# Two linear-attention layers on one core: four products multiplied straight out of PSUM, without filler products, under a new table of order

## The chip, the core and the metric

The kernel runs on one core of one Trainium2 chip. The metric is device time in microseconds (us) of one execution. The core has five instruction queues that matter here: TensorE (PE in the profile, with its weight loads as PEld), ScalarE (ACT), VectorE (DVE), GpSimd (POOL) and SyncE (SP, which here only issues DMAs). Products land in PSUM; everything else works in SBUF.

## The reference

The input `x` is 2048 tokens of 512 values, with 32 heads of 16. Two kinds of layers follow each other twice, each behind a layernorm without weights and with a residual add:

```python
x = A_x
x = x + _A_ref(_layernorm(x), ...)     # layer 0, A
x = x + _B_ref(_layernorm(x), ...)     # layer 0, B
x = x + _A_ref(_layernorm(x), ...)     # layer 1, A
x = x + _B_ref(_layernorm(x), ...)     # layer 1, B
```

A cuts the tokens into 4 segments of 512. In each it does causal softmax attention, and mixes in what a running memory of the earlier segments gives. B has no mask and no segments:

```python
pq = jnp.einsum('bhsd,hdf->bhsf', q, w_phi)
pk = jnp.einsum('bhsd,hdf->bhsf', k, w_phi)
phi_q = jnp.concatenate([_softmax(pq), _softmax(-pq)], axis=-1)
phi_k = jnp.concatenate([_softmax(pk), _softmax(-pk)], axis=-1)
kv = jnp.einsum('bhsf,bhsd->bhfd', phi_k, v)
z = jnp.einsum('bhsf->bhf', phi_k)
num = jnp.einsum('bhqf,bhfd->bhqd', phi_q, kv)
den = jnp.einsum('bhqf,bhf->bhq', phi_q, z)[..., None] + 1e-06
o = num / den                           # then @ wo
```

So B's queries need the sums `kv` and `z` over all 2048 tokens before any of them can be multiplied out. That is why the kernel ends with a stage that has only the queries of the second layer B in it.

## The kernel before

**Tiles.** The tokens lie in 16 tiles of 128 (tile `t`), four to a segment or chunk `c`. `X`, the running sum, stays in SBUF from the first load to the last store. PSUM is used through a few buffers; the four large ones of a pool `pD`, 128 x 1024 in f32 each (`D` in the profile), hold nearly all products that somebody must then copy, exponentiate, multiply or add.

**Order.** The program is written as a graph of operations. Each has the tiles it reads and writes, and one engine or two that may run it. `Graph.place` gives every operation a place in one total order, an engine, and every tile a buffer. All three come out of a table, the string `ORDER`, which is packed in base 85 and says nothing to a reader. `emit` then writes each engine's program in that order, with a semaphore wait wherever an operation needs another engine's result or a buffer that another engine still uses. Each engine runs its own program strictly in order, so an instruction that waits holds all that stand behind it on its engine. SP's queue holds the DMA transposes (line 383) and the stores (line 387) in the same manner.

**The stages.** Layer A of the first layer goes segment by segment (`a_proj`, `a_att`, `out_proj`), each followed by `b_keys`, which adds the segment's keys to `kv` and `z` (products "KV", the running sum on DVE, and at the last one `Rkv` of line 943). Then `b_query` of each chunk of the first layer overlaps layer A of the second. The second `b_query` has nothing behind it: it is the end of the program, from about 424 us on.

**`b_query`.** For a chunk of four tiles PE makes the query products, ACT exponentiates them into `EQ` (lines 366, "qexp"), PE makes the denominators, and DVE and ACT turn them into the weights `AB`. Then each tile has a chain of its own: PE's numerators `N` in PSUM; their multiplication by the weights on DVE into `Tm`; the sum of the two halves of `Tm`, on DVE or POOL ("nadd"); a transpose of that, mostly by a DMA from SP; the output products on PE (line 356); the residual add into `X` out of PSUM on DVE (line 926); and, in the second layer, the store. The multiplication has two forms:

```python
if (L, t) in COPIED:
    Ns = self.T(self.p2, "T")
    self.act(lambda Ns=Ns: Ns.t[:], lambda N=N: N.t[:], ACT.Copy, 1024, [N], [Ns], label="Nev")
    v(lambda e, ...: e.tensor_tensor(shape(Tm.t[:]), shape(Ns.t[:]), w(), ALU.mult), 600, ...)    # line 1087
else:
    v(lambda e, ...: e.tensor_tensor(shape(Tm.t[:]), shape(N.t[:]), w(), ALU.mult), 1131, ...)    # line 1090
```

In the first, ACT copies `N` to SBUF as bf16 (through a helper, so its line in the profile is 366), and DVE multiplies from there. In the second, DVE reads `N` out of PSUM itself. `COPIED` has all 16 tiles of the second layer and tiles 0 to 3 of the first. Tiles 0 and 15 of the second layer (`PE_T`) have no sum and no DMA: PE transposes and adds their two halves, and an eviction follows. Tiles 14 and 15 (`SOLO`) have output products of their own; the others go in pairs.

**Other lines that the prediction names.** Line 341 and line 356 are PE's products, 356 those of the projections and of `kv`. Lines 374 and 375 are copies out of PSUM by ACT or DVE. Lines 590 and 591 are a tile's layernorm statistics, line 605 a small step of the same. Line 878 divides layer A's products out of PSUM, and line 882 adds the memory's part, on DVE or POOL ("oadd"). Line 795 is a step of the memory's part, line 1007 weights the values for `kv`, line 650 belongs to the feature map of A's keys, line 541 is a step of the gates at the start. Line 662 is the warm-up of PE at the start.

**Filler products.** `keep` (line 671 on) makes two products of a constant with itself into a buffer of `pD`, which nobody reads. Six of them stand among the other operations of the last stage; the row of their twelve products is at line 678.

Of the kernel before, what the change touches and what calls it, by code (L numbers as in the profile page):

```python
# [16 lines left out]
D = 512  # L17
H = 32
# [294 lines left out]
class Kernel:  # L313
# [149 lines left out]
    def T(self, pool, cls):  # L463
        return Tile(pool, cls)
# [206 lines left out]
    def keep(self):  # L671

        D = self.T(self.pD, "S")

        def fn(e):
            for hf in range(2):
                r = self.onesb[64 * hf:64 * hf + 64, :]
                ins = e.matmul(D.t[:, 512 * hf:512 * hf + 512], r, r[:, None, :].to_broadcast([64, 4, 128]), start=True, stop=True, tile_position=(64 * hf, 0))
            return ins
        self.g.op({"pe": (215.0, fn)}, [self.R("onesb")], [D], label="keep", rows=64)  # L680

# [421 lines left out]
    def build(self):  # L1103
        R = self.R
# [9 lines left out]
        for L in range(2):  # L1114
            if L == 0:
# [7 lines left out]
                g0 = next(o for o in self.g.ops[n0:] if o.label == LATER[0])  # L1123
# [4 lines left out]
            for s in range(NSEG):  # L1128
# [5 lines left out]
                for i0 in (0, 2):  # L1134
                    t = s * 4 + i0
# [11 lines left out]
        for _ in range(N_KEEP):  # L1147
            self.keep()
# [21 lines left out]
COPIED = {(L, t) for L in range(2) for t in range(16) if L or t < 4}  # L1170
HALVED = set()
N_WARM = 16
N_KEEP = 6
# [4 lines left out]
c-rlG1GFYtlWpMm8fDwIZQHhO+qP}n=q}rAn`L%ab=S-MZdXt9|9jTVd+W_wli$7hWu9{~V#kghk(u{qfQFD5k^n<eNCu6dF*JchkQ&lJIzUJPDIpbPg!E7oN<u9FC<w  # L1178
Ko4iE%^fKpHz3PEA02xXuw)P<(d44Oj=XbG*LHMD`Y&<-j=d*}cip$HU(%1{OBK_18jouD&xfpSnDia}MV2F0NS)Q1Xi4X(otXaJ|+4%~#ia2n3Q1*i@ZG+czP&<$!pI
J}45L4ko`&;uNtg<jAT`okyK7y7_V7!I>wB#eLvm;<BW9Gr)K&>Py~Y`6rM;R;-ZOwb-PLvFYWqag>}g0%1{-iEO-2Hu1B;RE;(+F=L$4D&-OOpS9P9>&M7a3VCsMmP@  # L1180
^zzv)a1E4O}!-dch7r|m!0{I{d41}AQ6*^%WOpBed3w{q#@RV}G=a>RhVggKv@!=jkfcr2Bp3z4z2<qct_!xrWQ%HmwKY<3g43<I?Ooz#E2xP#-m>iShExe5x@k@9JUq
N~t4_$F6bi<z53o~J690wr~2?ia0jg7GhT3ikjpgZ=!6_5pMV;y`>D<KHC!xjjIrq~CwK{I?GKfp)u1x&%Im>s@`V4Mt}!wj5>{V)UzV-f6&q4*7a1{+`sJcjkq8=K=d
_$_9|7MKkIXW?vYjrkFg(ZXgZfL*975w^h|)CyZ-Ps)xtup8yXT-YB6;8xfMyP!LT!H4(}#)E>m8>YfE_!y@{F&u(<aTDah@9=xfjfHR(48<8x9K&!Fj>ddg6iZ-9EQR
# [90 lines left out]
```

## Time and profile before

| | |
|---|---|
| median of 3 runs | 463.37 us (462.33 to 463.4) |
| the profiled execution | 462.93 us, of which the profile's span is 461.2 |
| mean granted clock of TensorE in it | 0.998 |
| busy: PE, DVE, ACT, POOL | 437.7, 416.2, 420.3 and 80.1 us |
| HBM read and written | 6.32 MB and 2.10 MB |

Busy time is the time in which an engine had an instruction running. The page's slices give the same over time, a fortieth of the span (11.5 us) to a digit:

```profile
PE   8989899899999999998899999999999999998896
...
DVE  6989998898889999898999899998899889998896
ACT  4999999899999998789699999999999999878991
POOL 2402021101221211102532031130221023110020
```

Rows of the groups (lines) have: line, engine, operation, what it writes and reads with its shape, count; then busy time and the mean of one in ns; then the engine's idle time before such instructions and who ended it. Rows of a timeline have: start, duration, engine, line, operation, tiles; and in square brackets the wait before it with the instruction that ended it. Rows of a chain have: start, duration, and the instruction or transfer that held the next one.

### The profile page before, as it was taken

How to read it: one execution, taken by the hardware profiler on the slowest of the kernel's cores; microseconds unless marked ns; L12 is line 12 of the kernel's file. 1: busy time of each engine (PE TensorE's matmuls, PEld its weight loads, DVE VectorE, ACT ScalarE, POOL GpSimd, SP SyncE). 2: the span in 40 equal slices, each digit the busy share in tenths (PEclk: the TensorE clock that was granted, in tenths of full speed). 3: DMA queues.
4: the chain of work that ended last, by engine and by line, in shares of the span. 5: the costliest groups of instructions: out<-in, count | busy, mean ns of one | idle time of the engine just before them, and what ended most of it. 6: DMA issues, size and time to landing. Idle time of an engine off the chain costs nothing.

```text
span 461.2 us, 25354 instructions
## 1 busy us (share of the span) xinstructions
PE 437.7 (95%) x11716; PEld 295.6 (64%) x11716; DVE 416.2 (90%) x807; ACT 420.3 (91%) x542; POOL 80.1 (17%) x160
## 2 busy tenths in 40 slices
PE   8989899899999999998899999999999999998896
PEld 4456667667776776675456677677677677666553
DVE  6989998898889999898999899998899889998896
ACT  4999999899999998789699999999999999878991
POOL 2402021101221211102532031130221023110020
PEclk9999999999999999999999999999999999999999
DMA  8554642552233322100243443264113321200357
GB/s 247 127 150 80 127 63 37 75 96 54 50 46 54 46 40 36 37 3 4 48 54 78 71 85 72 49 96 61 26 39 49 50 39 27 48 14 1 50 121 180
DMA packets 90058, 30.37 MB, mean 66 GB/s; under 512 B 76640, under 2 KB 89952, under 8 KB 89952
## 3 DMA queue, kind: packets, MB, share of 16 engines
q1 hardware_dynamic: 89520, 28.48, 33.3%
q8 instruction: 92, 1.51, 1.4%
q10 hardware_dynamic: 432, 0.27, 0.2%
q14 instruction: 14, 0.11, 0.1%
HBM read 6.32 MB, written 2.10 MB: 18 GB/s over the span
## 4 chain that ended last, share of the span: by engine, by line
PE 48%; ACT 40%; DVE 6%; DMA 3%; issue 2%; SPq 0%
PE D L356 31%; ACT p L366 21%; PE D L341 15%; ACT pF L366 13%; ACT pE L366 5%; DMA p<-p 2%; PE D L662 2%; DVE X L926 1%; DMA X<-in_A_x_dram 1%; DVE p L1090 1%; DVE p L375 1%; DVE stats L590 1%; ACT pS L366 1%; DVE p L611 0%; DVE pK L375 0%
## 5 line engine op out<-in xcount | busy, mean ns | idle before, releaser
L366 ACT ACTIVATE p<-D 128x1024 bf16<-128x1024 f32 (+2 forms) x224 | 216.0, 1004 | 13.5 <-PE D L356 9.7
L366 ACT ACTIVATE pF<-D 128x896 bf16<-128x896 f32 x128 | 116.7, 940 | 2.8 <-PE D L341 2.5
L341 PE MATMUL D<-pK,pQ 64*128 64x256 bf16 (+3 forms) x1536 | 112.9, 243 | 4.1 <-ACT pF L366 1.0
L341 PEld LDWEIGHTS D<-pK,pQ 64*128 64x128 bf16 x1536 | 55.2, 94 | 40.7 <-ACT pF L366 5.4
L341 PE MATMUL D<-pV,pF 64*128 64x34 bf16 x1024 | 73.8, 175 | 0.4 <-ACT p L366 0.4
L341 PE MATMUL D<-pW,pF 64*128 64x34 bf16 x1024 | 71.3, 175 | 0.0
L341 PEld LDWEIGHTS D<-pV,pF 64*128 64x128 bf16 x1024 | 55.3, 93 | 2.3 <-ACT p L366 0.7
L341 PE MATMUL D<-pV,p 64*128 64x34 bf16 x1024 | 53.3, 176 | 0.3 <-issue 0.2
L366 ACT ACTIVATE pE<-D 128x768 bf16<-128x768 f32 x64 | 52.3, 831 | 1.4 <-PE D L341 1.0
L341 PEld LDWEIGHTS D<-pW,pF 64*128 64x128 bf16 x1024 | 51.9, 93 | 0.9
L341 PE MATMUL D<-pW,p 64*128 64x34 bf16 x1024 | 52.1, 176 | 0.0
L598 POOL TENSOR_SCALAR rstd<-mv 128x1 f32<-128x1 f32 x60 | 16.1, 272 | 205.9 <-DVE mv L591 205.5
L341 PEld LDWEIGHTS D<-pV,p 64*128 64x128 bf16 x1024 | 47.0, 93 | 3.3 <-issue 0.9
L341 PE MATMUL D<-tri,two 64*128 64x128 bf16 (+1 forms) x384 | 46.7, 234 | 0.4 <-issue 0.4
L341 PEld LDWEIGHTS D<-pW,p 64*128 64x128 bf16 x1024 | 45.2, 93 | 1.3
L590 DVE BATCH_NORM_STATS2 stats<-X 128x6 f32<-128x512 bf16 x64 | 42.9, 680 | 3.0 <-DMA X<-in_A_x_dram 2.5
L341 PE MATMUL D<-pV,pE 64*128 64x34 bf16 x512 | 44.9, 175 | 0.4 <-issue 0.4
L926 DVE TENSOR_TENSOR X<-X,D 128x1024 bf16<-128x1024 bf16 (+1 forms) x36 | 39.4, 1095 | 5.7 <-PE D L356 5.0
L341 PE MATMUL D<-pW,pE 64*128 64x34 bf16 x512 | 42.5, 175 | 0.1
L985 DVE TENSOR_REDUCE pS<-p 128x64 f32<-128x1024 bf16 (+1 forms) x36 | 38.8, 1088 | 1.8 <-ACT p L366 1.8
L375 DVE CAST p<-D 128x512 bf16<-128x512 f32 x48 | 31.1, 683 | 6.3 <-PE D L356 6.1
L356 PE MATMUL D<-WB_o,p 64*128 64x512 bf16 (+1 forms) x288 | 33.0, 353 | 2.7 <-issue 1.3
(115 smaller groups left out, 988.9 us busy)
## 6 DMA issues: line engine op xcount, KB each, us to landing
pW<-pV SPq DMA_DIRECT2D x16, 136.0 KB, 3.1
out_dram<-X SPq DMA_DIRECT2D x7, 256.0 KB, 2.8
X<-in_A_x_dram SPq DMA_DIRECT2D x3, 512.0 KB, 6.1
pX<-in_B_wqkv_dram SPq DMA_DIRECT2D x3, 512.0 KB, 4.6
p<-p SPq DMA_TRANSPOSE x76, 2.8
pX<-p SPq DMA_TRANSPOSE x54, 3.2
WA_k<-in_A_wk_dram SPq DMA_DIRECT2D x2, 256.0 KB, 6.3
WA_q<-in_A_wq_dram SPq DMA_DIRECT2D x2, 256.0 KB, 7.0
```

The costliest lines, as they stand in the source:

```text
L341: ins = e.matmul(out_ap, lhsT, rhs, start=st, stop=sp, tile_position=(basep(lhsT), basep(out_ap)))
L356: ins = e.matmul(out_ap, lhsT[64 * hf:64 * hf + 64], rhs[64 * hf:64 * hf + 64], start=k == 0 and i == 0, stop=k == 1 and i == len(lists[hf ...
L366: return self.g.op({"act": (dur, lambda e: e.activation(out_ap(), in_ap(), func, scale=scale))}, reads, writes, opens, label=label)
L375: "dve": ((340 if fast else n / 0.96 + 65), lambda e: e.tensor_copy(out_ap(), in_ap()))}
L590: v(lambda e: e.bn_stats(self.stats[:, t, :], self.X[:, t, :]), 602, [R("X", t)], [R("st", t)], label="bn")
L598: v(lambda e: e.tensor_scalar(rs, self.mv[:, t, 1:2], LN_EPS, None, op0=ALU.add), 170, [R("mv", t)], [R("rstd", t)], eng="pool", label="rstd")
L662: ins = e.matmul(D.t[c0:, r0 * 8:r0 * 8 + n], r[:, c0:], ones(r, n), start=True, stop=True, tile_position=(r0, c0))
L926: self.v(lambda e: e.tensor_tensor(X(), X(), src(), ALU.add), 65 + 512 * n / 0.96, pr + xr, xr, label="res")
L985: fn = lambda e, sgn=sgn, eo=eo, Z=Z, n=n: e.tensor_reduce(Z.t[:, 0:64 * n].rearrange("p (k s h) -> p k s h", k=n, s=2)[:, :, sgn, :], eo( ...
L1090: v(lambda e, N=N, Tm=Tm, w=w, shape=shape: e.tensor_tensor(shape(Tm.t[:]), shape(N.t[:]), w(), ALU.mult), 1131, [N, AB[(0, 0)], AB[(0, 1) ...
```

## The change

`COPIED` loses every fourth tile of the second layer: 3, 7, 11 and 15. Their numerators are multiplied by DVE out of PSUM, and four copies of ACT are gone. `keep` and its six calls are gone. The table `ORDER` is a new one. It moves instructions on all engines, most by a few places, and changes the engine of some: of the sums of line 1093, eight go from DVE to POOL and one comes back; of the sums of line 882, four go and two come back; several copies out of PSUM change between ACT and DVE, as many in one direction as in the other. In all, DVE has 798 operations in place of 807, ACT 540 in place of 544, POOL 165 in place of 156, and PE six fewer. From the place of `keep` on, a line of the new kernel has a number lower by 11, from `COPIED` on by more.

```diff
@@ -667,17 +667,6 @@
...
-    def keep(self):
-
-        D = self.T(self.pD, "S")
-
-        def fn(e):
-            for hf in range(2):
-                r = self.onesb[64 * hf:64 * hf + 64, :]
-                ins = e.matmul(D.t[:, 512 * hf:512 * hf + 512], r, r[:, None, :].to_broadcast([64, 4, 128]), start=True, stop=True, tile_position=(64 * hf, 0))
-            return ins
-        self.g.op({"pe": (215.0, fn)}, [self.R("onesb")], [D], label="keep", rows=64)
...
@@ -1144,8 +1133,6 @@
...
-        for _ in range(N_KEEP):
-            self.keep()
         self.g.place(self.pools, ORDER)
...
@@ -1167,72 +1154,71 @@
...
-COPIED = {(L, t) for L in range(2) for t in range(16) if L or t < 4}
+COPIED = {(L, t) for L in range(2) for t in range(16) if L == 1 and t % 4 != 3 or L == 0 and t < 4}
...
-N_KEEP = 6
...
 ORDER = """
-c-rlG1GFYtlWpMm8fDwIZQHhO+qP}n=q}rAn`L%ab=S-MZdXt9|9jTVd+W_wli$7hWu9{~V#kghk(u{qfQFD5k^n<eNCu6dF*JchkQ&lJIzUJPDIpbPg!E7oN<u9FC<w
...
+c-rlH1(Y4fl4U@0Gl-d)nVFfHnVFfHnVFdxZ80<00$VbOWsq#imNZo@>96f?&w9MOXJ^mZ>h6N9sK^^PZp6#?`o)I?kOq=NU8o23p#e06M$j0V00Tl(Xa-3jDFCE^gg_
...
```

Where the prediction shows rows of an order, they are an engine's instructions in the order of its program: line, operation, tile written and tiles read, shape, and xN for N like ones in a row.

More of the change, by code (lines that the diff above doesn't have):

```diff
@@ L1180 @@
[L1180 to L1183, printed above, removed]
@@ L1233 @@
[L1233 to L1235 removed]
+c-rlH1(Y4fl4U@0Gl-d)nVFfHnVFfHnVFdxZ80<00$VbOWsq#imNZo@>96f?&w9MOXJ^mZ>h6N9sK^^PZp6#?`o)I?kOq=NU8o23p#e06M$j0V00Tl(Xa-3jDFCE^gg_
+7g0#ZS0NC}CcDinokP#y9@4JZc1As^(2vQQJ6LknmLt)MlufwoWrN<ukk2kk*Z0VoLNp#s!`oS>l;l!ii37&<^M$N{;bA{2p8s05Xv3e<)=PzE}}F*puq;1XPhc+d$H8
```

110 lines of the change are left out of this document (56 added, 54 removed).

## The prediction

> **What bounds the kernel now.** I read the page's busy times first, then the chain of waits, then busy time by stretch, then the timelines of DVE, ACT and SP where the chain leaves PE and ACT.
>
> ```profile
> PE 437.7 (95%) x11716; PEld 295.6 (64%) x11716; DVE 416.2 (90%) x807; ACT 420.3 (91%) x542; POOL 80.1 (17%) x160
> PE 48%; ACT 40%; DVE 6%; DMA 3%; issue 2%; SPq 0%
> ```
>
> Three engines are above 90%, and the chain changes between PE and ACT all the time: no engine alone is the bound. So the question is stage by stage which one is full.
>
> ```profile
> 120.00:140.00 20.00, 19.58 (x638) 14.46 (x632) 18.51 (x35) 19.94 (x27) 4.20 (x6) 1.00 0.33 48
> 320.00:340.00 20.00, 19.99 (x520) 13.46 (x516) 18.09 (x30) 20.00 (x26) 3.47 (x4) 1.00 0.23 44
> 426.00:451.00 25.00, 21.36 (x598) 12.73 (x592) 22.36 (x48) 23.46 (x37) 2.43 (x2) 1.00 0.44 84
> 451.00:461.20 10.20, 6.57 (x88) 3.36 (x84) 6.74 (x8) 0.60 (x1) 0.00 (x0) 0.92 0.74 190
> ```
>
> The columns are the stretch, its length, then busy time of PE, weight load, DVE, ACT and POOL, the granted clock and DMA. In the attention stages (first two rows) ACT has nothing idle, and the change takes no work from it there. In 426 to 451 us, where the second layer B's queries are multiplied out, ACT is busy 23.46 of 25.00 us and DVE 22.36: both full. After 451 nobody is full: the kernel waits. For what, the end of the chain says:
>
> ```profile
> 444.81 3.96 DMA p<-p
> ...
> 453.12 3.71 DMA p<-p
> 456.83 0.04 issue
> 456.88 0.63 PE D L356 x8
> ...
> 458.21 0.69 DVE X L926
> ```
>
> A DMA transpose (`p<-p`, the transposed sum of tile 14) of 3.71 us holds the last output products, the last residual add ends at 458.90, and the store follows. The queue of SP and DVE's row show why it is so late:
>
> ```profile
> 452.10 0.58 SPq L387 DMA_DIRECT2D out_dram<-X  x1
> 453.12 1.19 SPq L383 DMA_TRANSPOSE p<-p  x1
> 454.37 4.90 SPq L387 DMA_DIRECT2D out_dram<-X  x6
> ...
> 449.85 1.28 DVE L1087 TENSOR_TENSOR p<-p,pS 128x1024 bf16<-128x1024 bf16 x2
> 451.17 0.42 DVE L1093 TENSOR_TENSOR p<-p 128x512 bf16<-128x512 bf16 x1
> 451.51 1.21 DVE L926 TENSOR_TENSOR X<-X,D 128x1024 bf16<-128x1024 bf16 x1
> ```
>
> DVE had the sum at 451.59, but SP first issued a store of other tiles at 452.10, the transpose only at 453.12, and it landed at 456.83.
>
> **The change part by part.** *The four multiplications.* These groups have the prices:
>
> ```profile
> L366 ACT ACTIVATE p<-D 128x1024 bf16<-128x1024 f32 x208 | 208.8, 1044 | 12.3 <-PE D L356 9.4 <-PE D L341 1.8
> ...
> L375 DVE CAST p<-D 128x512 bf16<-128x512 f32 x48 | 31.1, 683 | 6.3 <-PE D L356 6.1
> ...
> L1090 DVE TENSOR_TENSOR p<-D,pS 128x1024 bf16<-128x1024 f32 x12 | 14.5, 1214 | 0.1
> ...
> L1087 DVE TENSOR_TENSOR p<-p,pS 128x1024 bf16<-128x1024 bf16 x20 | 13.5, 689 | 0.6 <-ACT p L366 0.5
> ...
> L1093 POOL TENSOR_TENSOR p<-p 128x512 bf16<-128x512 bf16 x10 | 12.3, 1231 | 65.1 <-DVE p L1090 33.2 <-DVE p L1087 31.6 <-DVE nb L605 0.2
> ...
> L1093 DVE TENSOR_TENSOR p<-p 128x512 bf16<-128x512 bf16 x16 | 6.8, 422 | 0.1
> ...
> L678 PE MATMUL D<-onesb 64*128 64x512 bf16 x12 | 2.1, 378 | 0.4 <-ACT p L366 0.4
> ```
>
> ACT loses 4 x 1.044 = 4.2 us in the last part and takes over one eviction that DVE had (0.6). DVE pays 4 x (1.214 - 0.689) = +2.1. The new table moves four of the last part's sums (line 1093) from DVE to POOL and one back, 3 x 0.422 = -1.3, and the eviction saves 0.68. DVE's account is +2.1 - 1.3 - 0.7 = +0.1 us: nothing. ACT gets 3.6 us of slack, but it is not what ends last any more: DVE, with 22.36 us of work in 25.00, is. Idle time of DVE of at most 2.6 us is all that ACT's slack could give back. I take none of it for the multiplications themselves: DVE ends its last one at about 451.2, as now. The row behind it then decides.
>
> *The end of the program.* On DVE, the last multiplications (p<-p,pS from ACT's copy; p<-D,pS out of PSUM), sums (p<-p) and residual adds (X<-X,D), as they stand before:
>
> ```order
> L1087 TENSOR_TENSOR p<-p,pS 128x1024 x2
> L1093 TENSOR_TENSOR p<-p 128x512
> L926 TENSOR_TENSOR X<-X,D 128x1024 x3
> L926 TENSOR_TENSOR X<-X,D 128x512
> L926 TENSOR_TENSOR X<-X,D 128x1024
> L926 TENSOR_TENSOR X<-X,D 128x512
> ```
>
> The same stretch now:
>
> ```order
> L1082 TENSOR_TENSOR p<-p 128x512
> L1076 TENSOR_TENSOR p<-p,pS 128x1024
> L1079 TENSOR_TENSOR p<-D,pS 128x1024
> L915 TENSOR_TENSOR X<-X,D 128x1024 x4
> L915 TENSOR_TENSOR X<-X,D 128x512 x2
> ```
>
> Tile 14's multiplication now stands ahead of tile 15's direct one, and its sum has gone to POOL. On SP's queue (transposes p<-p and stores out_dram<-X), the end before:
>
> ```order
> L383 DMA_TRANSPOSE p<-p 128x4x128 x6
> L387 DMA out_dram<-X 128x2x512
> L383 DMA_TRANSPOSE p<-p 128x4x128
> L387 DMA out_dram<-X 128x2x512 x3
> L387 DMA out_dram<-X 128x512
> ```
>
> The same end of SP's queue now:
>
> ```order
> L383 DMA_TRANSPOSE p<-p 128x4x128 x5
> L387 DMA out_dram<-X 128x2x512
> L383 DMA_TRANSPOSE p<-p 128x4x128 x4
> L387 DMA out_dram<-X 128x2x512 x5
> L387 DMA out_dram<-X 128x512 x2
> ```
>
> The last transpose no longer stands behind a store. With these durations:
>
> ```profile
> p<-p SPq DMA_TRANSPOSE x76, 2.8
> ...
> L926 DVE TENSOR_TENSOR X<-X,D 128x1024 bf16<-128x1024 bf16 x28 | 34.0, 1215 | 4.2 <-PE D L356 3.5
> ...
> L926 DVE TENSOR_TENSOR X<-X,D 128x512 bf16<-128x512 bf16 x8 | 5.4, 676 | 1.5 <-PE D L356 1.5
> ```
>
> If DVE ends tile 15's direct multiplication at 451.2, it ended tile 14's at 450.0; POOL's sum takes 1.23 (0.42 on DVE, a loss of 0.8 on this path), so 451.2; issue to landing is 2.8 by the median, so 454.0 in place of 456.83. The transpose is then no longer last. DVE's own row is: four adds of 1.215 and two of 0.676 from 451.2 are 6.2, to 457.4 (a little less, since DVE's instructions overlap in the timeline: 451.17 + 0.42 against 451.51). The last add ended at 458.90. Gain 1.5 to 1.9; I take 1.6. Bounds: 0, if DVE arrives 1.6 later than now; 2.9, if it gets back half of its 2.6 us of idle time before that.
>
> *The filler products* are 2.1 us of PE (line 678), and PE has 3.6 us idle beside them in 426 to 451: it waits there in any case, so nothing is gained. What they may hide is a rival below.
>
> *The start.* DVE once waits for data:
>
> ```profile
> 24.54 0.16 DVE L541 TENSOR_TENSOR gt<-gt 128x32 f32<-128x32 f32 x1
> 26.23 0.69 DVE L590 BATCH_NORM_STATS2 stats<-X 128x6 f32<-128x512 bf16 x1 [1.53 <-DMA X<-in_A_x_dram]
> ...
> 28.66 0.81 ACT L366 ACTIVATE pE<-D 128x768 bf16<-128x768 f32 x1 [0.73 <-PE D L341]
> ```
>
> Statistics of tile 13 stand there before tile 13 has been loaded, and the evictions of the next segment's products (pK<-D) queue behind them. DVE at this place before (pK<-D: the evictions, BN_STATS: the statistics of one tile):
>
> ```order
> L541 TENSOR_TENSOR gt<-gt 128x32
> L590 BN_STATS stats<-X 128x6
> L375 CAST pK<-D 128x512 x2
> L591 BN_AGGR mv<-stats 128x2
> L375 CAST p<-D 128x512 x3
> ```
>
> The same evictions and what now stands around them:
>
> ```order
> L375 CAST pV<-D 128x32x16 x2
> L590 BN_STATS stats<-X 128x6
> L650 TENSOR_TENSOR p<-p 128x1024
> L375 CAST pK<-D 128x512 x2
> L591 BN_AGGR mv<-stats 128x2
> ```
>
> The statistics in the new place are of tile 8, loaded long before. What the 1.53 us cost is ACT's idle 0.73 behind them at most, since ACT is full before and after. Bounds 0 and 0.73; I take 0.4.
>
> *The rest.* The table permutes nearby instructions everywhere. Where ACT is full, this can lose and hardly win. One misplaced product cost ACT 1.46 us once:
>
> ```profile
> 92.42 0.92 ACT L366 ACTIVATE pF<-D 128x896 bf16<-128x896 f32 x1 [1.46 <-PE D L341]
> ```
>
> I bound the rest by one such wait in either direction, and take 0.
>
> *Sum.* The profiled execution took 462.93 us (span 461.2). 462.93 - 1.6 - 0.4 = 460.9. The median of the runs is 463.37, 0.44 above it; so the forecast is 461.3, and with all bounds at their ends 458.3 to 464.8.
>
> **The rivals.** *Slower: POOL's sums hold DVE.* The new table gives POOL nine sums more in all: seven of line 1093, two of line 882. Where POOL and DVE meet, the trace has this:
>
> ```profile
> 383.91 1.53 POOL L882 TENSOR_TENSOR p<-p 128x512 bf16<-128x512 bf16 x1 [8.02 <-DVE p L795]
> ...
> 384.92 1.07 DVE L1007 TENSOR_TENSOR pT<-p,pT 128x1024 bf16<-128x1024 bf16 x1
> ...
> L1007 DVE TENSOR_TENSOR pT<-p,pT 128x1024 bf16<-128x1024 bf16 x32 | 21.6, 695 | 0.4
> ```
>
> The DVE instruction with both inputs in SBUF took 1.07 and not 0.695 while POOL's sum ran to 385.44: 0.38 more. Nine such collisions of 0.38 give 461.3 + 3.4 = 464.7; the five sums of the last part, each holding DVE for its whole 1.23, give 467.5; I price it between, 466.1. It decides once DVE is held for more than 3.5 us in all. Against it: behind the last sum's multiplication DVE's next instruction reads PSUM (p<-D,pS), and two others have X<-X,D next; a PSUM multiplication beside POOL's sum looks like the very use of the direct tiles. Chance 0.16. The Trainium skill (SBUF — State Buffer, Who interferes with whom) makes this a rule that speaks against the change: DVE with two SBUF inputs and a GpSimd instruction that reads SBUF exclude each other, and the second waits for the whole first. By that rule every sum on POOL would be worth moving only beside a PSUM reader; the trace agrees in the row of 1.07.
>
> *No change: the gain is given back.* DVE reaches its last multiplication 1 to 1.5 us later because it must now wait for PE's product and PSUM in place of ACT's copy, or one wait of ACT in the attention stages grows as at 92.42. Then 463.0. For it: DVE and ACT are both full up to 451, and one slipped step there is not made good. Chance 0.22.
>
> *The clock drops without fillers.* From 424 on PE does mostly small products.
>
> ```profile
> 424.00:427.40 3.40, 2.11 (x132) 1.76 (x128) 2.61 (x6) 3.28 (x6) 0.00 (x0) 1.00 0.02 5
> 456.20:459.60 3.40, 1.37 (x18) 0.62 (x16) 1.93 (x3) 0.00 (x0) 0.00 (x0) 1.00 0.98 323
> 459.00:460.00 1.00, 0.00 (x0) 0.00 (x0) 0.00 (x0) 0.00 (x0) 0.00 (x0) 0.79 0.98 339
> ```
>
> PE busy 1.37 of 3.40 us was followed by a granted clock below 1.00; 2.11 was not. Half clock for one such stretch costs PE 1.7 us at most, and DVE's work covers part: 463.0. I see no stretch in the new order with as little as 1.37, so 0.06. The Trainium skill (TensorE: Matmul & The Clock Gate, What's actually happening) has the clock halve only after an idle window of 3.4 us; by that it could not fall here at all. The row says a window 40% busy was enough, so the measurement is the stricter.
>
> **How the numbers follow.** The forecast has 0.56. About 0.3% is what a measurement of this kernel can tell: 461.98 to 464.76 counts as no change. Faster 0.57 (the forecast, with a few parts of the other cases); slower 0.21 (the port, and a fifth of "given back" that goes past 464.76); the rest, 0.22, the same. The likeliest case alone, with the end's gain between 1.0 and 2.9 and the start's between 0 and 0.7, spans 459.8 to 462.4. For 8 in 10 the range must take in "given back" and the cheap end of the port: 459.3 to 465.2.
>
> **What would show it.** Right: the last transpose is issued before the stores and lands by about 454; the last 6 us before the final store are back-to-back residual adds on DVE; ACT has idle time of some 3 us in 426 to 451; DVE's 1.53 us wait for X near 25 us is gone. Wrong: DVE instructions of p<-p,pS longer than 0.69 beside POOL's; a granted clock under 1.00 between 424 and 450; or the last part starting a microsecond or more later than in this row:
>
> ```profile
> 426.39 0.41 PE L341 MATMUL D<-Rkv,p 64*128 64x64 bf16 x16 [0.23 <-DVE Rkv L943]
> ```

## The result and the profile after

| | before | after |
|---|---|---|
| median, 15 runs each, taken together | 462.87 us (460.96 to 463.88) | 464.86 us (463.29 to 470.21) |
| ratio after/before | | 1.0062 [1.0041, 1.0082] |
| the profiled execution, its span | 462.93, 461.2 us | 464.75, 463.0 us |

The change makes the kernel 0.6% slower. The forecast was 461.3, faster. The time lies inside the range (to 465.2), on the wrong side of before.

The page of after, busy times and the engines' shares of the chain:

```profile
PE 439.3 (95%) x11704; PEld 295.8 (64%) x11704; DVE 416.3 (90%) x798; ACT 417.7 (90%) x538; POOL 89.5 (19%) x169
...
PE 58%; ACT 26%; DVE 10%; DMA 2%; issue 2%; POOL 1%; SPq 0%; DVEq 0%; ACTq 0%
```

ACT is relieved (417.7 busy against 420.3, and 26% of the chain against 40%), and PE has taken its place: 58% against 48%, although PE has six operations fewer. DVE's account came out as worked (416.3 against 416.2).

Busy time by stretch, after, the last stage to 451 us (columns as in the prediction):

```profile
424.00:451.00 27.00, 23.25 (x640) 14.38 (x636) 24.19 (x49) 23.33 (x36) 5.01 (x4) 0.87 0.45 73
```

The same stretch of before:

```profile
424.00:451.00 27.00, 22.30 (x654) 13.54 (x650) 24.29 (x52) 25.43 (x39) 2.43 (x2) 1.00 0.40 78
```

ACT's idle time rose from 1.57 to 3.67 us, by 2.1 where the forecast worked out 3.6, and bought nothing. The granted clock is 0.87 in place of 1.00. PE's timeline of after, where the sums over all keys (`Rkv`) are first used:

```profile
426.77 0.40 PE L341 MATMUL D<-Rkv,p 64*128 64x64 bf16 x16
```

DVE's timeline of after, its end:

```profile
450.67 0.68 DVE L1076 TENSOR_TENSOR p<-p,pS 128x1024 bf16<-128x1024 bf16 x1
451.27 1.22 DVE L1079 TENSOR_TENSOR p<-D,pS 128x1024 bf16<-128x1024 f32 x1
452.41 3.47 DVE L915 TENSOR_TENSOR X<-X,D 128x1024 bf16<-128x1024 bf16 x3
457.20 2.60 DVE L915 TENSOR_TENSOR X<-X,D 128x1024 bf16<-128x1024 bf16 x3 [1.32 <-PE D L356]
```

SP's queue of after, its end:

```profile
448.82 0.57 SPq L387 DMA_DIRECT2D out_dram<-X  x1
449.51 5.46 SPq L383 DMA_TRANSPOSE p<-p  x4
455.02 5.16 SPq L387 DMA_DIRECT2D out_dram<-X  x7
```

These rows, with those of before in the prediction, divide the 1.8 us between the two spans:

| stretch | before | after | difference |
|---|---|---|---|
| start to the first `Rkv` product | 426.39 | 426.77 | +0.38 |
| from there to the end of the last multiplication (451.13; 452.49) | 24.74 | 25.72 | +0.98 |
| to the end of the last residual add (458.90; 459.80) | 7.77 | 7.31 | -0.46 |
| to the end of the span | 2.30 | 3.20 | +0.90 |

The forecast had -0.4, 0, -1.6 and 0 here. Every term came out worse, by 0.8 to 1.1 us each. The first row needs care: the profiles are single executions. Over the seven profiles of this case that run before's program up to there, the first `Rkv` product starts at 423.5 to 427.0 us, on average at 425.2; before's 426.39 is a late one. So +0.38 understates what the body of the program lost.

### The profile page after: what moved, and what is told of

Its sections match the earlier page's. It is cut to its first block, busy times and chain, and to the rows that moved or that the text cites. A ratio compares the mean times of both kernels' runs of the same rounds, so it can differ in the third digit from the quotient of the medians.

```text
span 463.0 us, 25325 instructions
## 1 busy us (share of the span) xinstructions
PE 439.3 (95%) x11704; PEld 295.8 (64%) x11704; DVE 416.3 (90%) x798; ACT 417.7 (90%) x538; POOL 89.5 (19%) x169
## 4 chain that ended last, share of the span: by engine, by line
PE 58%; ACT 26%; DVE 10%; DMA 2%; issue 2%; POOL 1%; SPq 0%; DVEq 0%; ACTq 0%
PE D L356 38%; PE D L341 20%; ACT p L366 13%; ACT pF L366 8%; ACT pE L366 3%; DMA p<-p 2%; DVE stats L590 2%; DVE X L915 2%; DVE p L1079 1%; DVE p L1076 1%; DMA X<-in_A_x_dram 1%; DVE p L375 1%; DVE p L867 1%; POOL rstd L600 0%; DVE p L611 0%
## 5 line engine op out<-in xcount | busy, mean ns | idle before, releaser
L366 ACT ACTIVATE p<-D 128x1024 bf16<-128x1024 f32 (+2 forms) x220 | 213.0, 1007 | 13.9 <-PE D L356 8.4
L600 POOL TENSOR_TENSOR rstd<-rstd,mhalf 128x1 f32<-128x1 f32 x60 | 35.7, 602 | 3.2
```

The lines of the kernel that those rows point to most:

```text
L366: return self.g.op({"act": (dur, lambda e: e.activation(out_ap(), in_ap(), func, scale=scale))}, reads, writes, opens, label=label)
L600: v(lambda e: e.tensor_tensor(rs, rs, self.mhalf[:], ALU.pow), 540, [R("rstd", t), R("mhalf")], [R("rstd", t)], eng="pool", label="rstd")
```

## The experiments

Each ratio is to the kernel before, run beside it on the same chip; the groups of runs were on different chips, so kernels of different groups are compared by these ratios alone. "Fillers" are the six filler products, "body" is the program up to about 421 us, "tail" what stands behind it. At that point both tables have finished exactly the same operations, so a table can be cut there and continued with the other.

### Were the fillers missed, and is the direct form the loss?

The clock did fall. Busy time by stretch of after, in stretches of 3.4 us:

```profile
424.40:427.80 3.40, 2.58 (x164) 2.10 (x160) 2.25 (x7) 3.09 (x6) 0.00 (x0) 1.00 0.02 5
427.80:431.20 3.40, 2.50 (x96) 2.12 (x96) 2.61 (x7) 3.37 (x7) 0.00 (x0) 0.50 0.02 5
431.20:434.60 3.40, 3.05 (x58) 1.90 (x60) 3.40 (x9) 2.90 (x6) 1.15 (x1) 0.50 0.19 39
```

Two stretches at half clock follow one in which PE was busy 2.58 of 3.40 us. So the first four runs gave after its fillers back, took before's away, and put each multiplication form into the other's order:

```diff
# e1_after_fillers: after
+        for _ in range(N_KEEP):
+            self.keep()                      # six, all between 424 and 431 us
# e2_before_nofill: before
-        for _ in range(N_KEEP):
-            self.keep()
# e3_before_direct: before's order; one filler moved
-COPIED = {(L, t) for L in range(2) for t in range(16) if L or t < 4}
+COPIED = {(L, t) for L in range(2) for t in range(16) if L == 1 and t % 4 != 3 or L == 0 and t < 4}
# e4_after_copies_fillers: e1 with COPIED as in before (ACT's four copies back)
```

> The changed kernel with its six filler products back, all between 424 and 431 us of its profile (one behind the last exponentials' products, two ahead of tile 4's denominators, two ahead of tile 2's numerators, one ahead of tile 10's). Theory 1, the clock: the profile of the changed kernel has the granted clock at 0.50 from 427.8 to 434.6 us, behind a stretch of 3.41 us in which PE streamed little; with fillers the clock stays at 1.00 there, the products of 0.61 us are 0.40 again, and the kernel takes 1.5 to 2.5 us less than the changed one: 0.996 to 1.001 of before. Theory 2, the new order and the direct multiplications themselves: the clock stays up, but the time does not move: 1.005 to 1.007 of before. In between, both.

Measured: 1.0060 [1.0036, 1.0084]; in its profile the clock is 1.00 all through. DVE's timeline, the last multiplication:

```profile
451.30 1.22 DVE L1090 TENSOR_TENSOR p<-D,pS 128x1024 bf16<-128x1024 f32 x1
```

and PE's, the first `Rkv` product:

```profile
427.50 0.40 PE L341 MATMUL D<-Rkv,p 64*128 64x64 bf16 x16
```

From one to the other are now 25.02 us in place of after's 25.72: the fallen clock costs 0.7 us of that stretch. But the whole kernel is as slow as after (1.0062). The two intervals would hide 0.7 us, which is 0.15%; they would not hide 0.6%. The clock is a real effect, and it is not the cause of the whole loss.

> The kernel before without its six filler products, all else as it was. Theory 1, the clock: from about 425 us on the granted clock falls to 0.50 for one or two steps of 3.41 us, and the time goes to 1.002 to 1.006 of before. Theory 2: the fillers were 2.1 us of PE time for nothing; the clock may or may not fall, the time stays within 0.1% of before, or is less.

Measured: 1.0010 [0.9997, 1.0024]. Without fillers before loses nothing that can be told; in its profile the clock stayed at 1.00 up to 457 us.

> The kernel before, its order and its fillers, with only the four copies of ACT gone and DVE multiplying these tiles out of PSUM at the same place in its row (one filler stands some places earlier). Theory of the prediction: DVE pays 2.1 us in a stretch in which it is 89% busy, ACT has 4.2 us less; without the new table's moves of sums to POOL DVE becomes the later one: 1.001 to 1.004 of before. Rival: DVE had waited for ACT's copies, so it gets its 2.1 us back: 0.998 to 1.000.

Measured: 1.0118 [1.0101, 1.0135], slower than either side expected. The waits of DVE in the last stage of this kernel:

```profile
DVE p L1087 <- ACT p L366: 3.4, 3, 1.8
```

In before the same row is 0.3 us, once:

```profile
DVE p L1087 <- ACT p L366: 0.3, 1, 0.3
```

In before's order a direct tile keeps its PSUM buffer until DVE comes to it, where ACT's copy had freed it early. PE's waits of e3 show it, 6.2 us in all that before does not have, and then ACT's copies of later tiles are late and DVE waits for them:

```profile
PE D L341 <- DVE p L1090: 3.4, 2, 2.6
PE D L356 <- DVE p L1090: 2.8, 2, 1.5
```

The longest of them, on PE's timeline:

```profile
434.59 0.61 PE L341 MATMUL D<-Rkv,p 64*128 64x64 bf16 x16 [2.59 <-DVE p L1090]
```

The granted clock also fell in this profile, to 0.50 for 3.41 us each from 424.3, 434.5 and 448.2 on, although the fillers are there; no run tells how the 1.2% divides between the waits and the clock.

> The changed kernel with both put back: six fillers (as in the run with fillers alone) and the four copies of ACT, each right behind its tile's numerators, under the new order. So it does before's work in the new order. If the direct multiplications gain by themselves, it is slower than the changed kernel with fillers by 0.5 to 2 us (ACT has 4.2 us more in a stretch where it was full before). If they lose, it is faster than that one by up to 2 us. If it stands at 1.000 of before, the new order by itself moves nothing.

Measured: 1.0107 [1.0087, 1.0127], against 1.0060 with the direct form. So the direct form alone loses 1.2% in the old order, and taking it back out of the new order loses another 0.5%: order and form belong together, and the new order with its own form still loses 0.6%. e3 and e4 have four runs each.

### Body or tail?

```diff
# h1_oldbody_newtail:  ORDER = before's up to ~421 us, then after's (direct, no fillers)
# h2_newbody_oldtail:  ORDER = after's up to ~421 us, then before's (copies, fillers)
# h3_newfirst_oldrest: ORDER = after's up to ~206 us, then before's (copies, fillers)
# h4_oldbody_newtail_fillers: h1 with the six fillers
```

> The program cut at about 421 us, where both tables have finished the same operations: before's order, engines and buffers up to there, the changed kernel's behind it, with the four direct multiplications and without fillers. Theory 3, the body: what the run with fillers left unexplained (0.6% at full clock) is lost in the first 421 us, in which the new table moved sums to POOL and permuted everything. Then this kernel stands at 0.999 to 1.002 of before. Theory 4, the last part: the new order of the queries' stage loses it; then 1.004 to 1.007. Half each would be 1.002 to 1.004.

Measured: 1.0037 [1.0018, 1.0056].

> The other way round: the changed kernel's order, engines and buffers up to about 421 us, before's behind it, with before's four copies and six fillers. Theory 3, the body: 1.004 to 1.007 of before. Theory 4, the last part: 0.999 to 1.002. Together with the kernel of old body and new last part it should add up to the changed kernel, if nothing else plays.

Measured: 1.0105 [1.0074, 1.0136]. In its profile the clock was at 0.50 for 3.41 us in the body, near 228 us, and again behind the first `Rkv` product, although its tail is before's, with the fillers:

```profile
428.90:432.30 3.40, 3.08 (x129) 2.51 (x122) 2.59 (x8) 3.40 (x9) 0.00 (x0) 0.50 0.02 5
432.30:435.70 3.40, 3.40 (x46) 1.49 (x40) 2.86 (x7) 3.05 (x6) 0.00 (x0) 0.50 0.39 77
```

So the six fillers do not keep the clock up in every execution.

> The changed kernel's table only for the first layer's A and keys, up to about 206 us (where the start with its 1.53 us wait of DVE lies, and five of the seven changes of engine), before's for all behind it. The prediction's gain at the start of 0.4 us would give 0.999. Theory 3, if the loss lies in the first layer: 1.003 to 1.006; if in the second: 1.000.

Measured: 1.0045 [1.0026, 1.0063].

> As the kernel of old body and new last part, with the six fillers in the last part. What it gains over that one is the price of the fallen clock: by the products that took 0.61 in place of 0.40 us in the changed kernel's profile 1 to 2 us if they are on the path (0.996 to 0.998 of it), nothing if DVE and ACT hide them.

Measured: 1.0061 [1.0040, 1.0083], no better than h1 without fillers.

The tail loses 0.4% on its own, and the first 206 us of the table, in which no multiplication changes its form, lose 0.45% on their own. The parts do not add up to after's 0.6%: h2 alone stands above it. What h2 has more of the new table than h3 is the part between 206 and 421 us, and it costs 0.6% more; but after, with the same body and its own tail, stands at 1.0062. Why is open.

### The body: PE stops where a block of its program begins

The prediction named no wait of the body. PE's waits in after, those that no semaphore explains ("issue"):

```profile
PE D L356 <- issue: 4.0, 5, 1.8
...
PE D L341 <- issue: 1.2, 4, 0.4
```

In before these rows are 3.1 and 1.6; in e2, the same body, line 356 has only

```profile
PE D L356 <- issue: 1.1, 3, 0.4
```

PE's timeline of after shows the two largest:

```profile
33.52 0.23 PE L356 MATMUL D<-pV,p 64*128 64x136 bf16 x2 [1.79 <-issue]
...
51.10 0.35 PE L356 MATMUL D<-pV,p 64*128 64x136 bf16 x6 [1.07 <-issue]
```

Counted over PE's records from the start (products, weight loads and the few others), the stops between 24 and 424 us stand at instructions 961, 1985, 2753, 4033, 8897, 16321 and 16833: each is 193 above a multiple of 256. In the 17 profiles of this case there are 87 such stops of more than 0.15 us, and 85 of them stand at 193; the other two are one and the same product, in e2 and i3. The page's queues show what has that size:

```profile
q8 instruction: 92, 1.51, 1.4%
```

92 packets of 16.4 KB: PE has 2 x 11,704 instructions, and 92 x 256 is 23,552. i3, a kernel below with 256 PE instructions more, has 93. I read these packets as PE's program in blocks of 256. Each of the stops in after ended 1.3 to 1.5 us after such a packet had landed; of the 85, 82 ended 1.2 to 1.6 us after one. The other three (in before, h4 and k1, up to 1.31 us long, all at instruction 4289) ended 2.2 to 2.4 us after it, so late landing alone does not explain them, and their cause is open. Over before and after, half of the packets begin within about 1.1 us of the moment PE passes the boundary before; I take that as the request. The block for 33.52 was asked for at 28.41 and came only from 30.88 to 32.26. What it met, by busy time by stretch of after (the last two columns are the DMA engines' share and GB/s; a packet counts whole in the stretch in which it starts, so the share can pass 1):

```profile
28.00:30.00 2.00, 2.00 (x122) 1.85 (x119) 1.95 (x5) 2.00 (x3) 0.00 (x0) 1.00 1.05 309
30.00:32.00 2.00, 1.74 (x31) 0.89 (x25) 1.84 (x5) 2.00 (x4) 0.00 (x0) 1.00 2.21 230
```

The same stretches of before:

```profile
28.00:30.00 2.00, 1.62 (x42) 0.95 (x42) 1.97 (x5) 1.34 (x2) 0.22 (x1) 1.00 0.71 237
30.00:32.00 2.00, 1.93 (x112) 1.64 (x106) 1.96 (x5) 1.84 (x3) 0.00 (x0) 1.00 0.03 8
```

And SP's queue of after, which fills the engines there:

```profile
24.91 0.62 SPq L474 DMA_DIRECT2D pX<-in_B_wqkv_dram  x1
25.58 1.00 SPq L474 DMA_DIRECT2D WA_o<-in_A_wo_dram  x2
26.62 0.43 SPq L474 DMA_DIRECT2D X<-in_A_x_dram  x1
27.09 0.97 SPq L474 DMA_DIRECT2D WA_o<-in_A_wo_dram  x2
29.19 4.80 SPq L383 DMA_TRANSPOSE pX<-pX  x3
```

Before has no stop near 33 us. The new table placed six load issues and three transposes just where PE runs through a block in 3.3 us (28.41 to 31.73) and needs the next one. The Trainium skill (Runtime: NRT & Kernel Launch, Instruction fetch mechanics) has a program refilled in blocks of 16 KiB, 256 instructions, and calls the cost of crossing into the next one "mostly hidden". The size agrees with the row of 92 packets. Between 24 and 424 us of after only 7 of some 85 crossings show a stop, but one of them costs 1.79 us.

There are two tests. If the count of instructions sets the places, a shift of everything by half a block must move the stops, and a shift by a whole block must not. The warm-up's products, whose results nobody reads, were cut into shorter ones:

```diff
# i2_before_shift128 (i3_before_shift256: all 16)
-            unit(128, 512, 1)
+            if k < 8:
+                unit(128, 57, 9)             # nine products of 57 columns: +128 PE instructions in all
+            else:
+                unit(128, 512, 1)
```

> The kernel before, with eight of its 16 warm-up products of 512 columns cut into nine of 57 columns each: 64 products, so 128 PE instructions, more at the start, the same columns, nothing else changed. Theory 5, the instruction stream: in every trace so far PE's unexplained stops lie at an instruction whose number has the remainder 193 when divided by 256, 1.2 to 1.7 us behind the landing of a 16 KB packet of the instruction queue; a block of 256 is asked for when PE enters the one ahead of it, and takes some 3.5 us (more where DMA engines are full) while PE needs as little as 3.5 us for 256 instructions. Then this shift puts the places of waiting onto other products: remainder 193 stays, the products at it change, stops grow in number and sum (estimate from the traces: 6 us more of them), and the time goes to 1.004 to 1.015 of before. Theories 3 and 4 without it (order of operations alone): 1.000 to 1.001, the 1 to 2 us of longer start aside, of which nothing shows since PE waits for data there.

Measured: 1.0225 [1.0189, 1.0261], above the expected range. Its profile is of the slowest of its six runs, 475.91 us where the median is 471.39; PE's timeline there has 12 stops from 24 to 424 us with 9.66 us in all, again all at 193. The longest:

```profile
61.29 0.20 PE L341 MATMUL D<-pV,p 64*128 64x34 bf16 x2 [2.32 <-issue]
```

> The same with all 16 warm-up products cut: 128 products, 256 PE instructions more. Theory 5: every later product stands at its old place in its block again, so the stops are those of before and the time is 0.999 to 1.002 of before, although twice as much has been added as in the kernel with 128. If the added start itself costs, this one is the slower of the two.

Measured: 1.0069 [1.0046, 1.0092], above the expected range too. Twice as many instructions were added, at a third of the cost: five stops with 1.84 us from 24 to 424 us, four of them at 193 and the largest at the product that stops in e2, and one of 2.27 us at 10.62, right behind the lengthened warm-up. That stop and a clock of 0.50 for 3.41 us behind it put PE 3.0 us behind before's profile by 18 us; at 419 us it is 2.8 behind. So the loss is that of the start, which the expected 0.999 to 1.002 had not counted.

The other test moves the traffic and not the boundaries. Six of SP's operations have another place; PE's program is untouched. SP's order, after against i1 (one load of `pX` comes from further down, outside this excerpt):

```diff
 L474 DMA pX<-in_B_wqkv_dram 128x4x512
-L474 DMA WA_o<-in_A_wo_dram 32x2x512 x2
 L474 DMA X<-in_A_x_dram 128x4x512
-L474 DMA WA_o<-in_A_wo_dram 32x2x512 x2
-L383 DMA_TRANSPOSE pX<-pX 128x4x128 x3
 L383 DMA_TRANSPOSE p<-p 128x4x128
+L383 DMA_TRANSPOSE pX<-pX 128x4x128
+L474 DMA pX<-in_B_wqkv_dram 128x4x512
+L383 DMA_TRANSPOSE pX<-pX 128x4x128 x2
+L474 DMA WA_o<-in_A_wo_dram 32x2x512 x4
```

i4_newfirst_loads_apart is h3 with the same moves, and k2_newbody_apart_oldtail is after's body with the moves and before's tail.

> The changed kernel with six of SP's operations moved: three transposes of weights, two loads of the first layer's output weights and one load of weights of layer B stand behind the first transposed sum of tile 0 (about 36 us) in place of ahead of it or later (25 to 45 us). Theory 5: the stop of PE at 33.5 us (1.8 us in the changed kernel's profile; its block was asked for at 28.4 us, when 1.3 MB of loads and three transposes kept the DMA engines full, and was fetched from 30.9 to 32.3) shrinks to under 0.5 us, that at 51.1 (1.1 us) perhaps too, and the time falls from 1.006 to 1.001 to 1.004 of before. If DMA traffic has no part in it, the stop stays and so does the time.

Measured: 1.0029 [1.0010, 1.0048], where after had 1.0062. Busy time by stretch of i1:

```profile
28.00:30.00 2.00, 2.00 (x122) 1.79 (x118) 1.96 (x5) 2.00 (x3) 0.00 (x0) 1.00 1.05 352
30.00:32.00 2.00, 1.76 (x32) 0.85 (x26) 1.84 (x5) 2.00 (x4) 0.00 (x0) 1.00 0.08 26
```

and its PE timeline:

```profile
32.50 0.23 PE L356 MATMUL D<-pV,p 64*128 64x136 bf16 x2 [0.74 <-issue]
```

The engines are free after 30 us (0.08 in place of 2.21), and the stop at that block falls from 1.79 to 0.74 us (under 0.5 was expected).

> The new table up to about 206 us with the same six moves on SP, before's order, copies and fillers behind it. Without the moves it stood at 1.0045 of before. Theory 5: without the long stops the new order of the first layer is the faster one (by the traces some 2 us if all stops are left out), so 0.996 to 1.001. Theory 3 without instruction fetch: 1.003 to 1.006 again.

Measured: 1.0002 [0.9977, 1.0027], where h3 had 1.0045.

> The new table up to about 421 us with the six moves on SP, then before's order, four copies and fillers. Theory 5: in the profile of the changed kernel with these moves the body ended some 0.9 us ahead of the traces of before's body, and before's last part is 0.4% faster than the new one by the kernel of old body and new last part; so 0.996 to 1.000. If the two parts of the table only fit one another: 1.003 or more, as the new body without the moves had 1.0105.

Measured: 1.0053 [1.0026, 1.0081] (without one run of 832 us), where h2 had 1.0105. The expected 1.000 was missed, though all three moved kernels gained. What k2 has more than i4 is again the table between 206 and 421 us, at 0.5%; their two profiles do not show it (first `Rkv` product at 426.08 and 425.99 us), and it stays open.

The gains from the six moves are 0.33, 0.43 and 0.52%, 1.5 to 2.4 us. Each gain alone is hardly wider than the two intervals it comes from, and the two kernels of each ran in different groups; all three point the same way. The sums of the stops between 24 and 424 us, one profile each:

| start of the program | kernels | stops, us | mean |
|---|---|---|---|
| before's | before 3.01, e2 0.70, e3 1.06, h1 1.36, h4 0.97, k1 3.08, k3 1.09 | 0.70 to 3.08 | 1.6 |
| after's | after 4.45, e1 4.96, e4 1.83, h2 3.16, h3 3.33 | 1.83 to 4.96 | 3.5 |
| after's, six operations moved | i1 2.18, i4 2.44, k2 2.40 | 2.18 to 2.44 | 2.3 |

The new table brings 1.9 us more of such stops, and the moves take 1.2 of them away again. That is a little over half of the 1.5 to 2.4 us that the moves gained. The rest is not shown; the moves also change when transposes and weights arrive. The length of the body agrees: with before's program the first `Rkv` product starts at 425.2 us on average (seven profiles), with after's at 426.5 (four, 424.3 to 427.5), with after's and the moves at 424.8 (two). The ranges overlap, so these are means of few samples: the body lost some 1.3 us, and the moves gave it back.

### The tail: the end does not shorten

The last four sums of after were ready at 448.64, 449.69, 450.75 (DVE) and 452.59 (POOL). But SP still had a store in its queue, and behind each issue of a transpose SP comes to the next only about 1.3 us later, so the four were issued at 449.51, 451.17, 452.45 and 453.76; the last landed at 456.21 and not at 454.0. If that store is what makes them late, moving it behind them must help:

```diff
# k3_oldbody_newtail_store_last: h1, SP's queue
-store of tiles 2, 3 ahead of the last four transposes
+store of tiles 2, 3 behind them
# k1_newtail_sum_on_dve: k3, and tile 14's sum (line 1082) on DVE in place of POOL
```

> Old body, new last part, with one store (tiles 2 and 3) moved on SP's queue from ahead of the last four transposes to behind them. Theory 6, SP's queue: the four transposes follow one another at 1.26 us each, so all of them are issued 0.6 us earlier, and the last residual add ends 0.4 to 0.6 us earlier: 0.9985 to 0.9995 of the kernel without the move (1.0037 of before). Rival, DVE's own row sets the end: no change.

Measured: 1.0071 [1.0046, 1.0096], against h1's 1.0037.

> As the kernel with the store moved, and the sum of tile 14 on DVE right behind its multiplication in place of POOL behind the next one. Theory 6: the transposes ahead in SP's queue decide, not the sum: within 0.1% of the kernel with the store moved, or slower by the 0.42 us that DVE pays. Rival, POOL's sum (1.15 us, and 0.1 us late) sets the last transpose: 0.5 to 0.8 us faster.

Measured: 1.0065 [1.0042, 1.0088].

Neither gained, but neither is a clean test of the store. Up to 9.4 us behind the first `Rkv` product DVE's rows of h1 and k3 agree to 0.01 us. Then k3 waits longer for PE, once by 0.73 and once by 0.40 us:

```profile
435.66 1.23 DVE L1079 TENSOR_TENSOR p<-D,pS 128x1024 bf16<-128x1024 f32 x1 [0.78 <-PE D L341]
438.03 1.22 DVE L915 TENSOR_TENSOR X<-X,D 128x1024 bf16<-128x1024 bf16 x1 [0.61 <-PE D L356]
```

PE's clock is at 0.50 for 6.83 us in both, but it fell 1.7 us behind the first `Rkv` product in h1, 4.0 in k3 and 2.9 in k1. So the price of a fallen clock in this stage depends on when it falls; from the first `Rkv` product to the last multiplication h1 takes 26.0 us, k3 and k1 some 27.1. Behind the last multiplication nothing was gained either, though k1 has what the prediction wanted, six adds with hardly a gap. Its DVE timeline:

```profile
453.97 3.47 DVE L915 TENSOR_TENSOR X<-X,D 128x1024 bf16<-128x1024 bf16 x3
457.65 2.60 DVE L915 TENSOR_TENSOR X<-X,D 128x1024 bf16<-128x1024 bf16 x3 [0.21 <-PE D L356]
```

The last add ends 6.19 us after the last multiplication, and the span ends 4.25 us after that. e4, with the old multiplications, has the six adds without any gap, and still the span (461.6) ends 3.58 us behind them:

```profile
451.89 6.13 DVE L926 TENSOR_TENSOR X<-X,D 128x1024 bf16<-128x1024 bf16 x6
```

Over the 17 profiles, the time from the last multiplication to the end of the span is 9.5 to 10.7 us in 16 (before 10.1, e2 9.8, e4 9.6, after 10.5, h1 10.3, k3 10.7, k1 10.4), whether the adds take 6.05 or 8.32; the seventeenth is h4 with 12.2, whose PE waited 2.91 us for a transposed sum and then ran at a clock of 0.50 for 3.41 us. What fills it, by busy time by stretch of after:

```profile
457.00:458.00 1.00, 1.00 (x22) 0.89 (x20) 0.80 (x1) 0.00 (x0) 0.00 (x0) 1.00 1.02 333
458.00:459.00 1.00, 0.91 (x18) 0.57 (x12) 0.91 (x2) 0.00 (x0) 0.00 (x0) 1.00 1.02 351
```

The DMA engines are full with stores while the last adds run. In after seven stores stand behind the last transpose, six in before; after's last store was issued at 459.83 and took 2.67 us to land, before's 1.80 (458.92 to 460.72). That adds which come sooner only wait longer as stores is what these numbers fit; a kernel that stores less at the end was not run.

The rest of the tail's loss lies ahead of the last multiplication. From the first `Rkv` product to it, the eight profiles with before's tail take 24.4 to 25.5 us, mean 24.8; after, h1 and i1 take 25.7 to 26.0, mean 25.9 (k1 and k3, above, some 27.1). To the end of the span it is 35.0 against 36.3. These 1.2 us (0.27%) are the tail's price, most of it in the multiplications. With fillers e1 and h4 take 25.0 there, so 0.8 of it is the fallen clock. Neither kernel was faster for them in the timed runs: 0.8 us are 0.17%, less than the intervals can tell. In the profiles e1's first `Rkv` product came 0.73 us later than after's, and h4's end took 1.9 us more than h1's. The body's 1.3 and the tail's 1.2 us are 0.5% together, of the 0.6% that were measured.

No kernel tried is faster than before; i4, level with it at 1.0002, is the nearest.

## Why the prediction was wrong

That 464.86 lies inside the range is luck: the range was widened for two rivals, and the loss came by other means.

**The start** (-0.4 forecast). The wait of 1.53 us went, and ACT's 0.73 behind it: ACT's timeline of after reaches the instruction that stood at 28.66 in before a microsecond earlier, and then loses it to PE's stop at 33.52.

```profile
27.62 0.82 ACT L366 ACTIVATE pE<-D 128x768 bf16<-128x768 f32 x1
...
34.05 0.92 ACT L366 ACTIVATE pF<-D 128x896 bf16<-128x896 f32 x1 [1.39 <-PE D L341]
```

So this term was right in kind and larger than forecast, and it was gone 6 us later.

**The rest** (0, bounded by one ACT wait of 1.46). This step failed first. It put at nothing a permuted order that it treated as many small moves of compute, and asked neither what SP's moved loads collide with nor what the "issue" waits of PE in before's own list were. These stops grew by 1.9 us (mean 3.5 against 1.6), and the body ended some 1.3 us later; h3 shows 0.45% for the first 206 us alone.

**The multiplications** (0). The sum for DVE was right (+0.1 us over the whole program); ACT's slack in the last stage grew by 2.1 us and not by 3.6. Putting the stage's length at unchanged failed: it took 0.98 us longer; with fillers it is 0.28, so 0.7 of it is the fallen clock, which the sum had at nothing.

**The end** (-1.6 forecast, -0.46 measured, and +0.90 behind it). The mechanism was right in part: no store stands directly ahead of the last transpose any more, and six adds end the program. Its price was wrong twice. I let the last transpose be issued when its sum was ready, at 451.2. The sum was ready at 452.59, since DVE came later, and I did not walk SP's queue, in which the last four stand 1.3 us apart: the transpose was issued at 453.76, and DVE waited 1.32 us for the products. And I carried before's 2.3 us from the last add to the end over unchanged. The row that speaks against it stood in the prediction: 456.20 to 459.60 of before, DMA share 0.98 at 323 GB/s, read there for its clock alone. From the last multiplication to the end the forecast allowed 8.5 us; the least of the 17 profiles is 9.5.

**The fillers** (0). Right as a sum: with them after is 1.0060, without 1.0062; before without them 1.0010. The rival on the clock had the wrong condition. I read off before that a window with PE 40% busy was needed; here one of 76% was enough, and a clock under 1.00 between 424 and 450 us was one of the prediction's own signs of being wrong. The Trainium skill (TensorE: Matmul & The Clock Gate, What's actually happening) has the clock halve after an idle window of about 3.4 us; the row at 424.40, with PE busy for 2.58 of 3.40 us, disagrees with that too.

**POOL's sums hold DVE** (0.16). The forecast was right to leave it out of the sum, but not because engines never meet. In the last stage POOL's timeline of after has

```profile
432.35 1.15 POOL L1082 TENSOR_TENSOR p<-p 128x512 bf16<-128x512 bf16 x1 [19.89 <-DVE p L1076]
435.02 1.54 POOL L1082 TENSOR_TENSOR p<-p 128x512 bf16<-128x512 bf16 x1 [1.52 <-DVE p L1076]
```

The second began while DVE was in a multiplication out of SBUF, and took 0.39 us longer than the first; DVE's two multiplications there keep their price, 1.28 for two that overlap a little:

```profile
434.26 1.28 DVE L1076 TENSOR_TENSOR p<-p,pS 128x1024 bf16<-128x1024 bf16 x2
```

Where POOL began first, DVE paid. There is one such case in after: a sum of POOL from 383.86 to 385.01, and beside it an instruction that takes 0.695 alone:

```profile
384.28 1.29 DVE L996 TENSOR_TENSOR pT<-p,pT 128x1024 bf16<-128x1024 bf16 x1
```

So whichever began second took longer, as the rule that the prediction named has it. The rival failed by its count: it priced five to nine collisions, and DVE was held once, for 0.6 us, much as in before (0.38). In the last stage four of the five sums began beside a DVE instruction that read PSUM.

**Given back** (0.22, 463.0). Nearest in kind, since what the end saved was lost elsewhere, but by other means and larger: the body's stops, the clock and the stores.

## What to carry to other kernels

A new order is not only an order of compute: where transfers are moved, they meet the blocks in which PE's own program arrives, and a wait called "issue" on the busiest engine is a row to be explained and not to be skipped. Before a gain at the end of a program is counted, the queue that issues the last transfers is walked entry by entry, with the time that each issue holds it, down to the last store, and with the traffic that the stores themselves need. And a direct form that saves another engine a copy also holds its buffer longer; here it was worth something only in the order that came with it (1.0060 against 1.0107 without it, and 1.0118 in the old order).

## What the runs showed of the hardware that was not expected

PE stops at fixed counts of its own instructions, 193 above a multiple of 256, for up to 2.32 us; 82 of 85 such stops ended 1.2 to 1.6 us after a packet of 16 KB had landed. 128 more instructions at the start cost 2.25%, 256 only 0.69%. SP issued after's last three transposes 1.3 us apart. A sum of POOL and a DVE instruction with both inputs in SBUF did not run side by side at full speed: the one that began second took 0.39 us (POOL) or 0.6 us (DVE) longer. And the clock fell to 0.50 for two stretches of 3.4 us behind one in which PE was 76% busy, while a stretch of before with 62% kept 1.00: the busy share alone does not tell which; what does stays open.
